# One 112-partition load of wq, and a result finished on 128 partitions with the gate applied last

## The chip, the cores and the metric

The kernel runs on one core of a Trainium2 chip. Five engines work side by side there: TensorE (PE in the profile; PEld is its weight load), VectorE (DVE), ScalarE (ACT), GpSimd (POOL) and SyncE (SP), which here only issues DMAs. The metric is the device time of one execution in microseconds; the time quoted for a kernel is the median of several runs.

## The reference

One token is decoded. An attention block over a long key and value cache and a small MLP mixer both read the same row `x` of 448 numbers, and a scalar gate mixes them:

```python
# x (1,1,448)   k_cache, v_cache (1,8,65536,256)   wq (448,4096)   wo (4096,448)   all bf16
q = (x @ wq).reshape(B, Sq, 16, 256).transpose(0, 2, 1, 3)
k, v = each of the 8 cached heads, used by 2 query heads
p = softmax(einsum("bhqd,bhkd->bhqk", q, k) * 256 ** -0.5)
a = einsum("bhqk,bhkd->bhqd", p, v).transpose(0, 2, 1, 3).reshape(B, Sq, 4096) @ wo
h = layernorm(x);  u = gelu(h (448) x w1 (1792) + b1);  b = u^T @ w2 + b2       # (1,1,448)
g = sigmoid((x * gate_w).sum(-1))
return g * a + (1 - g) * b
```

The caches are 2 x 268 MB, wq and wo 3.67 MB each. The caches are nearly all of the bytes.

## The kernel before

**Tiling.** The 8 heads of 65,536 keys are cut into 32 stages (`NP`) of 16,384 keys, four stages a head. A stage is one K load and one V load of 8.4 MB each, laid out as 128 partitions of 64 KB. K goes into a ring of one and a half stages (`kring`), V into one buffer (`vbuf`). The last K load and the first are cut in two halves, the last V load in four pieces.

**The engines in a stage.** A stage is eight chunks (`BODY`) of 2,048 keys. For each, PE transposes the keys into PSUM (L298), DVE and ACT copy them to SBUF (L569, L669), PE multiplies them with the two query columns (L318), ACT takes the exponential (L658). At the end of the stage PE sums the weights (L347) and multiplies them with V (L358). DVE and ACT also carry one step of the mixer in each of the first 14 stages. At the end of a head DVE takes the sums (`take`, L573 to L583), PE selects and projects with that head's rows of wo (L405) into `prj`, four column groups of 112 on the PSUM partitions 0, 32, 64, 96.

**The order of the DMAs.** SP issues all large loads on one queue, in program order: wq in two parts (L226, L228), K of stage 0 (L231, two halves), then, once q (`s_q`) and the broadcast layer norm (`s_hb`) are ready, V of stage 0 and the first rows of wo (L260). After that each K load waits until the first half of the stage before has been transposed (L237), and each V load until the stage before has finished with the buffer (L250). The last rows of wo go out after the last V pieces (L265). The small inputs come on ACT's queue (L638 to L643).

**wq before.** 448 rows don't divide by 128 partitions. `wq_a` takes the first 384 rows, three whole rows of 8 KB to a partition (24 KB); `wq_b` takes the last 64 rows, each cut in two halves, one half to a partition (4 KB). To match, PE turns `x` into columns `xcol`: three for the whole rows (L427) and two for the half rows, from a zero-padded copy `xrem` that DVE makes (L483, L490, L491, waited for by `s_xrem`). Then 32 column groups of q are each the sum of four matmuls, three of `wq_a` (L441) and one of `wq_b` (L443). wq lies in the V buffer, so V of stage 0 waits for q.

**Gate and mixer before.** `bcast` holds g, 1 - g and b2 on every partition. `take` multiplies the reciprocal of the softmax sum by g (L582), so what is projected is gated already. The mixer's sum gathers in the other half of the `prj` bank; once it is complete, after the seventh head, DVE copies it, adds b2 (L622 to L625), and signals `s_mix`. In the last stage PE waits for that and adds (1 - g) * b into `prj` with four one-row matmuls (L342), ahead of eight matmuls that only keep PE running (`spin`, L334).

**The end before.** After the last projection DVE and ACT copy two of the four column groups each to `out_row` on partition 0 (L634, L678), each copy adding 1 to `s_fin`; SP waits for 4 and writes one row of 896 bytes (L267).

```python
            eng.wait_ge(s_proj, H - 1)
            for h in range(REP):
                w = A_wo[(HQ - REP + h) * DH:(HQ - REP + h + 1) * DH, :]
                eng.dma_start(wo_sb[:, h, :], w.rearrange("(p j) n -> p (j n)", j=2)).then_inc(sem_wl[h], 16)
            eng.wait_ge(s_fin, NCG)
            eng.dma_start(out_ap, out_row[:, :]).then_inc(sem_out, 16)
```

Of the kernel before, what the change touches and what calls it, by code (L numbers as in the profile page):

```python
# [12 lines left out]
def bass_gated_mix__gqa_block_cached__mixer_token_mlp__decode_kernel(  # L13
# [40 lines left out]
    KTB = 2  # L54
    assert T % (CH * BODY) == 0 and PPH >= 2

    WF = 3
    REM = DM - WF * P
    assert 0 < REM and 2 * REM == P
    HALF = NQ // 2  # L60

# [28 lines left out]
    with ctx:  # L92
# [6 lines left out]
        def new_sem(name):  # L99
            return ctx.enter_context(nc.semaphore(name))  # L100
# [19 lines left out]

        early = vbuf[:, :, :].rearrange("p n d -> p (n d)")
        early_f = vbuf_f[:, :, :].rearrange("p n d -> p (n d)")
        wq_a = early[:, 0:WF * NQ].rearrange("p (j n) -> p j n", j=WF)
        wq_b = early[:, WF * NQ:WF * NQ + HALF]
        used = [WF * NQ + HALF]

        def scratch(rows, n, dt=bf16):
            o = used[0]
# [3 lines left out]

        wrows_b = scratch(3 * FT, P)
        identb = scratch(3 * FT, 3 * FT)
        xrem = scratch(1, 2 * P).rearrange("p (a n) -> p a n", a=2)
        xrow_b = scratch(1, DM)
        grow_b = scratch(1, DM)
        xcb_row = scratch(1, DM)
# [4 lines left out]
        scr_row = scratch(1, DM, f32)  # L143
        gu = sb([P, DM], bf16, "gu")
        w2cur = sb([P, 1], bf16, "w2cur")
        xcol = sb([P, WF + 2], bf16, "xcol")
        oTn = sb([P, 2 * REP], bf16, "oTn")
        accs = sb([P, SELC], f32, "accs")
        sel = sb([P, REP], f32, "sel")
# [10 lines left out]
        u_b = sb([P, DM], bf16, "u_b")  # L160
        z_b = sb([P, DM], bf16, "z_b")
        wtmp = sb([P, DM], bf16, "wtmp")
        out_row = sb([1, DM], bf16, "out_row")
        rest = sb([P, 1], bf16, "rest")
        bcast = sb([P, 3], f32, "bcast")
        brow1 = u_b[:, 0:WG]
        brow = z_b[:, 0:WG]
# [29 lines left out]
        s_d2a = new_sem("s_d2a")  # L197
        s_a2d = new_sem("s_a2d")
        s_col = new_sem("s_col")
        s_xrem = new_sem("s_xrem")  # L200
        s_xcol = new_sem("s_xcol")
        s_hrow = new_sem("s_hrow")
        s_h = new_sem("s_h")
# [3 lines left out]
        s_pb = new_sem("s_pb")  # L207
        s_oTn = new_sem("s_oTn")
        s_proj = new_sem("s_proj")
        s_mix = new_sem("s_mix")  # L210
        s_fin = new_sem("s_fin")
        sem_out = new_sem("sem_out")

        block = ctx.enter_context(nc.Block())

        x_row_ap = A_x.rearrange("a b c -> (a b) c")
        out_ap = out.rearrange("a b n -> (a b) n")

        def src(cache, j, n0=0, n1=NV):
            g, m = divmod(j, PPH)  # L220
# [3 lines left out]
        @block.sync  # L224
        def _(eng):
            eng.dma_start(wq_a.rearrange("p j n -> p (j n)"),  # L226
                          A_wq[0:WF * P, :].rearrange("(p j) n -> p (j n)", p=P)).then_inc(sem_wq, 16)
            eng.dma_start(wq_b, A_wq[WF * P:DM, :].rearrange("r (a n) -> (r a) n", a=2)  # L228
                          ).then_inc(sem_wq, 16)
            def load(dst, cache, j, n0, n1, at, sem):  # L230
                eng.dma_start(dst[:, at + n0:at + n1, :].rearrange("p n d -> p (n d)"), src(cache, j, n0, n1)  # L231
                              ).then_inc(sem, 16)

            for j in range(NP):
                last = j == NP - 1
                if j >= 1:
                    eng.wait_ge(sem_tr[NB - 1], BODY * (j - 1) + DC)  # L237
                if j == 0:
                    load(kring, A_k_cache, j, HV, NV, 0, sem_k)
                    load(kring, A_k_cache, j, 0, HV, 0, sem_kb)  # L240
                elif last:
                    load(kring, A_k_cache, j, 0, HV, HV, sem_k)
                    load(kring, A_k_cache, j, HV, NV, HV, sem_kb)
                else:
                    load(kring, A_k_cache, j, 0, NV, HV * (j % 2), sem_k)
                if j == 0:
                    eng.wait_ge(s_q, 1)
                    eng.wait_ge(s_hb, 1)
                else:
                    eng.wait_ge(sem_pv, j)  # L250
                load(vbuf, A_v_cache, j, 0, NFIRST if last else NV, 0, sem_v)
                if last:
                    for (n0, n1), sem in zip(pieces, sem_vp):
                        load(vbuf, A_v_cache, j, n0, n1, 0, sem)
                g, m = divmod(j, PPH)
                if m == 0 and g < H - 1:
                    if g >= 1:
                        eng.wait_ge(s_proj, g)
                    w = A_wo[g * REP * DH:(g + 1) * REP * DH, :]
                    eng.dma_start(wo_rows, w.rearrange("(p i) n -> p (i n)", i=2 * REP)).then_inc(sem_wo, 16)  # L260

            eng.wait_ge(s_proj, H - 1)
            for h in range(REP):
                w = A_wo[(HQ - REP + h) * DH:(HQ - REP + h + 1) * DH, :]
                eng.dma_start(wo_sb[:, h, :], w.rearrange("(p j) n -> p (j n)", j=2)).then_inc(sem_wl[h], 16)  # L265
            eng.wait_ge(s_fin, NCG)
            eng.dma_start(out_ap, out_row[:, :]).then_inc(sem_out, 16)  # L267
            eng.wait_ge(sem_out, 16)

        @block.gpsimd  # L270
# [11 lines left out]
        def _(pe):  # L282
# [53 lines left out]

            def values(j, c0, u16):
                with pe.If(j == NP - 1):
                    pe.wait_ge(s_mix, 1)
                    for q in range(NCG):  # L340
                        r = slice(32 * q, 32 * q + 1)
                        pe.matmul(prj[r, 0:WG], rest[r, :], brow[r, :], start=False, stop=True,  # L342
                                  skip_group_check=True)
                    spin(8)
                pe.wait_ge(sem_exp, c0 + (BODY + 2))
                for r in range(BODY):
# [76 lines left out]
            pe.wait_ge(sem_ident, 1)  # L423
            pe.wait_ge(sem_x, 16)
            for j in range(WF):
                pe.matmul(acc[:, j:j + 1], xrow_b[0:1, j:WF * P:WF], one, start=True, stop=True)
            pe.wait_ge(s_xrem, 2)  # L427
            for a in range(2):
                pe.matmul(acc[:, WF + a:WF + a + 1], xrem[0:1, a, :], one, start=True, stop=True)
            pe.wait_ge(sem_misc, 16 * 5)  # L430
            pe.matmul(acc[:, WF + 2:WF + 2 + 3 * FT], wrows_b, identb, start=True, stop=True).then_inc(s_col, 1)  # L431

            pe.wait_ge(s_xcol, 1)
            pe.wait_ge(sem_wq, 32)
            for dj in range(2):
                for h in range(HQ):
                    j = dj * HQ + h
                    col = h * DH
                    a, cb = divmod(col, HALF)
                    for kt in range(WF):  # L440
                        pe.matmul(sps[:, 1, j:j + 1], wq_a[:, kt, col + dj:col + DH:2],  # L441
                                  xcol[:, kt:kt + 1], start=(kt == 0), stop=False)
                    ins = pe.matmul(sps[:, 1, j:j + 1], wq_b[:, cb + dj:cb + DH:2],  # L443
                                    xcol[:, WF + a:WF + a + 1], start=False, stop=True)
            ins.then_inc(s_q, 1)
            pe.wait_ge(s_hrow, 1)
            pe.matmul(prj[:, 0:DM], ones_sq[0:1, :], h_row, start=True, stop=True)
# [32 lines left out]
        def _(vec):  # L480
            for b in range(0, NB, 2):
                vec.sem_inc(sem_ev[b], 1)
            vec.memset(xrem, 0.0)  # L483
            vec.memset(zrow[:, :], 0.0)
            vec.wait_ge(sem_ident, 1)
            vec.tensor_copy(identb, ident[0:3 * FT, 0:3 * FT]).then_inc(s_xrem, 1)
            vec.reduce_sum(sel[:, :], ident[:, :].rearrange("p (j n) -> p n j", j=4)[:, 0:REP, :], axis=AX.X)
            vec.wait_ge(sem_x, 16)
            vec.drain()
            vec.tensor_copy(xrem[0:1, 0, 0:P:2], xrow_b[0:1, WF * P:DM])  # L490
            vec.tensor_copy(xrem[0:1, 1, 1:P:2], xrow_b[0:1, WF * P:DM]).then_inc(s_xrem, 1)  # L491
            vec.tensor_copy(xrow, xrow_b)
            vec.drain()
            vec.reduce_sum(stat[:, 0:1], xrow, axis=AX.X)
# [19 lines left out]
            vec.drain()  # L514
            vec.tensor_copy(statb[:, 4:5], stat[:, 3:4]).then_inc(s_d2a, 1)
            vec.wait_ge(s_col, 1)
            vec.tensor_copy(xcol[:, :], acc[:, 0:WF + 2]).then_inc(s_xcol, 1)
            vec.tensor_copy(params[:, :], acc[:, WF + 2:WF + 2 + 3 * FT]).then_inc(s_par, 1)
            vec.drain()
            vec.tensor_copy(w2p_b[:, :], params[:, 2 * FT:3 * FT])  # L520
            vec.wait_ge(s_a2d, 1)
# [47 lines left out]
                    vec.tensor_copy(ktT[:, k % KTB, b, :], kst_b[:, b, :]).then_inc(sem_ev[b], 1)  # L569

            def take(n, sem=sem_pv):  # L573
                vec.wait_ge(sem, n)
                vec.tensor_copy(accs[:, :], acc[:, 0:SELC]).then_inc(s_cp, 1)  # L575
                vec.drain()
                vec.reduce_sum(densum[:, :], accs[:, DENC:SELC].rearrange("p (nn hh) -> p hh nn", hh=REP),
                               axis=AX.X)
                vec.drain()
                vec.reciprocal(rden[:, :], densum[:, :])  # L580
                vec.drain()
                vec.tensor_scalar(rden[:, :], rden[:, :], bcast[:, 0:1], None, op0=ALU.mult)  # L582
                vec.drain()  # L583

            def by_head(src):
# [35 lines left out]
            vec.wait_ge(s_proj, H - 1)  # L621
            vec.tensor_copy(brow1, prj[:, WG:2 * WG])  # L622
            vec.drain()
            vec.tensor_copy(rest[:, :], bcast[:, 1:2])
            vec.tensor_scalar(brow, brow1, bcast[:, 2:3], None, op0=ALU.add).then_inc(s_mix, 1)  # L625
            with nc.Fori(NC - NCPH, NC, BODY, engines=on) as c0:
                for k in range(BODY):
                    evacuate(k, c0 + k)
# [1 line left out]
            vec.wait_ge(s_late, 1)  # L630
            by_head(sps[:, 0, 0:2 * REP])
            vec.wait_ge(s_proj, H)
            for q in range(0, NCG, 2):
                vec.tensor_copy(out_row[:, q * WG:(q + 1) * WG], prj[32 * q:32 * q + 1, 0:WG]).then_inc(s_fin, 1)  # L634

        @block.scalar
        def _(act):
# [25 lines left out]
            with nc.Fori(0, NP, 1, engines=OrderedEngineSet([act.engine])) as j:  # L663
# [9 lines left out]
                with act.If(j < FT):  # L673
                    act.wait_ge(s_u, j + 1)
                    act.activation(z_b[:, :], z_b[:, :], AF.Tanh).then_inc(s_tanh, 1)  # L675
            act.wait_ge(s_proj, H)
            for q in range(1, NCG, 2):
                act.activation(out_row[:, q * WG:(q + 1) * WG], prj[32 * q:32 * q + 1, 0:WG], AF.Copy  # L678
                               ).then_inc(s_fin, 1)


# [26 lines left out]
```

## Time and profile before

| what | value |
|---|---|
| median of 3 runs | 1266.1 us (1265.93 to 1266.6) |
| the profiled execution: its own time | 1266.1 us |
| its span, first to last instruction | 1264.0 us |
| bytes read from HBM | 544.22 MB, 431 GB/s over the span |
| busy: PE, PEld, ACT, DVE | 73%, 69%, 43%, 33% |
| second wq load: issued, last data packet ended | 1.20 us, 11.63 us after the span's start |
| first transpose of keys on PE | 27.4 us |
| last rows of wo landed, result's DMA issued | 1261.44 us, 1262.49 us |

A time after the span's start is counted from the first instruction. The profile says for each engine how long it was busy, for each group of instructions what ended the idle time before it, and for the whole span one chain: from the last instruction back to what released it, and so on. DMA packets are recorded one by one, with queue, start, duration and size. A load of 128 partitions shows 128 data packets and 16 packets of 4 bytes, one for each of the 16 DMA engines, that raise the semaphore.

### The profile page before, as it was taken

To read this page: it belongs to the slowest core of one execution; us is meant where nothing else is said; L and a number is where in the kernel's file an instruction comes from. 1 tells how busy PE (TensorE), PEld (TensorE's weight loads), DVE (VectorE), ACT (ScalarE), POOL (GpSimd) and SP (SyncE) were. 2 spreads that over 40 slices of the span, in tenths; PEclk is the share of its full clock that TensorE was granted. 3 is DMA by queue.
4 is the path that set the end of the run, shared out by engine and by line. 5 is a ranking of instruction groups with operands and counts; after the bars stand their busy time and mean duration, and the time that the engine had idled before them with its cause. 6 is when DMAs were issued, how large, how long until landed. Compare 5 with 4: busy or idle time off the path is not lost.

```text
span 1264.0 us, 38850 instructions
## 1 busy us (share of the span) xinstructions
PE 917.0 (73%) x17114; PEld 868.4 (69%) x17114; DVE 422.5 (33%) x764; ACT 538.2 (43%) x788; POOL 0.9 (0%) x7
## 2 busy tenths in 40 slices
PE   3876678766778667786676876758767688676688
PEld 2766668766677666786666876658766578666687
DVE  2433344333444333443222332323322233332233
ACT  1443345533355433454333553335533355433455
POOL 0000000000000000000000000000000000000000
PEclk9887788787898887987888987889887888877999
DMA  9999999999999999999999999999999999999998
GB/s 411 428 434 436 433 431 431 431 438 431 433 433 433 433 431 438 425 433 440 431 436 429 431 431 433 440 433 433 431 431 431 438 436 433 431 433 431 431 427 367
DMA packets 11623, 544.39 MB, mean 431 GB/s; under 512 B 1369, under 2 KB 1628, under 8 KB 2908
## 3 DMA queue, kind: packets, MB, share of 16 engines
q1 hardware_dynamic: 11522, 544.22, 99.7%
q8 instruction: 8, 0.13, 0.0%
q10 hardware_dynamic: 90, 0.01, 0.0%
q14 instruction: 3, 0.02, 0.0%
HBM read 544.22 MB, written 0.00 MB: 431 GB/s over the span
## 4 chain that ended last, share of the span: by engine, by line
DMA 70%; PE 29%; issue 1%; SPq 0%; DVEq 0%; DVE 0%; ACT 0%; ACTq 0%
DMA kring<-in_A_k_cache_dram 68%; PE kst L298 24%; PE sps L318 4%; DMA wo_sb<-in_A_wo_dram 2%; PE acc L358 0%; SPq L231 0%; SPq L265 0%; SPq L228 0%; SPq L226 0%; PE prj L405 0%; PE acc L347 0%; DVEq L92 0%; DVE out_row L634 0%; ACT pT L658 0%; ACTq L658 0%
## 5 line engine op out<-in xcount | busy, mean ns | idle before, releaser
L298 PE MATMUL kst<-ident,kring 128*128 128x128 f32 x4096 | 563.7, 299 | 304.9 <-DMA kring<-in_A_k_cache_dram 294.1
L669 ACT ACTIVATE ktT<-kst 128x1024 bf16<-128x1024 bf16 x512 | 500.0, 1021 | 667.3 <-PE kst L298 666.5
L298 PEld LDWEIGHTS kst<-ident,kring 128*128 128x128 f32 x4096 | 514.0, 156 | 314.8 <-issue 312.2
L569 DVE COPY ktT<-kst 128x1024 bf16<-128x1024 bf16 x512 | 354.2, 692 | 765.0 <-PE kst L298 742.0
L318 PEld LDWEIGHTS sps<-qcur,ktT 128*128 128x128 bf16 x8192 | 237.8, 96 | 4.1 <-issue 1.6
L318 PE MATMUL sps<-qcur,ktT 128*128 128x2 bf16 x8192 | 236.6, 163 | 1.3 <-issue 1.3
L358 PE MATMUL acc<-vbuf,pT 128*2 128x256 bf16 x4080 | 140.4, 305 | 3.8 <-issue 3.3
L358 PEld LDWEIGHTS acc<-vbuf,pT 128*2 128x2 bf16 x4080 | 105.2, 93 | 30.6 <-issue 3.8
L658 ACT ACTIVATE pT<-sps 128x32 f32 x256 | 51.8, 202 | 16.4 <-PE sps L318 16.4
L347 PE MATMUL acc<-pT,ones_sq 128*128 128x32 bf16 x256 | 11.7, 178 | 12.3 <-ACT pT L658 12.3
L347 PEld LDWEIGHTS acc<-pT,ones_sq 128*128 128x128 bf16 x256 | 8.6, 96 | 15.2 <-ACT pT L658 14.9
L675 ACT ACTIVATE z_b<-z_b 128x448 bf16<-128x448 bf16 x14 | 8.1, 577 | 20.5 <-DVE z_b L556 20.4
L575 DVE COPY accs<-acc 128x288 f32<-128x288 f32 x8 | 3.7, 458 | 38.5 <-PE acc L358 38.5
L394 PEld LDWEIGHTS acc<-sel,accs 128*64 128x64 f32 x112 | 10.8, 214 | 0.9
L394 PE MATMUL acc<-sel,accs 128*64 128x1 f32 x112 | 11.4, 260 | 0.0
L431 PE MATMUL acc<-vbuf 42*128 42x42 bf16 x1 | 0.2, 214 | 8.3 <-DMA b_b<-in_B_b_dram 8.3
L405 PE MATMUL prj<-wo_sb,oTn 128*1 128x112 bf16 x128 | 3.7, 244 | 3.1 <-DVE oTn L600 2.9
L431 PEld LDWEIGHTS acc<-vbuf 42*128 42x128 bf16 x1 | 0.1, 102 | 8.4 <-DMA b_b<-in_B_b_dram 8.4
L562 DVE TENSOR_TENSOR gu<-wtmp,z_b 128x448 bf16<-128x448 bf16 x14 | 5.5, 393 | 1.0
L554 DVE TENSOR_TENSOR z_b<-u_b,wtmp 128x448 bf16<-128x448 bf16 x14 | 5.5, 393 | 1.0
L550 DVE TENSOR_TENSOR z_b<-wtmp,u_b 128x448 bf16<-128x448 bf16 x14 | 5.5, 393 | 1.0
L548 DVE TENSOR_TENSOR wtmp<-u_b 128x448 bf16<-128x448 bf16 x14 | 5.5, 392 | 1.1
(89 smaller groups left out, 82.5 us busy)
## 6 DMA issues: line engine op xcount, KB each, us to landing
kring<-in_A_k_cache_dram SPq DMA_DIRECT2D x4, 4096.0 KB, 24.3
vbuf<-in_A_v_cache_dram SPq DMA_DIRECT2D x1, 6144.0 KB, 25.7
wo_sb<-in_A_wo_dram SPq DMA_DIRECT2D x7, 448.0 KB, 27.6
vbuf<-in_A_wq_dram SPq DMA_DIRECT2D x1, 3072.0 KB, 10.2
vbuf<-in_A_v_cache_dram SPq DMA_DIRECT2D x1, 1024.0 KB, 27.8
vbuf<-in_A_v_cache_dram SPq DMA_DIRECT2D x1, 768.0 KB, 28.9
vbuf<-in_A_wq_dram SPq DMA_DIRECT2D x1, 512.0 KB, 10.9
vbuf<-in_A_v_cache_dram SPq DMA_DIRECT2D x31, 29.7
```

The costliest lines, as they stand in the source:

```text
L298: ins = pe.transpose(kst[:, b, i * P:(i + 1) * P], kring_f[:, at + NT * (k % DC) + 4 * b + i, :], ident[:, :])
L318: ins = pe.matmul(sps[:, par, 2 * nt:2 * nt + 2], ktT[:, par, b, ntl * DH + dj:(ntl + 1) * DH:2], qcur[:, dj, :], start=(dj == 0), stop=(d ...
L347: pe.matmul(acc[:, DENC:SELC], ones_sq[:, :], pT[:, r, :], start=False, stop=(r == BODY - 1), skip_group_check=True)
L358: ins = pe.matmul(acc[o:o + REP, 0:DH], pT[:, r, 2 * nt:2 * nt + 2], vbuf[:, n, :], start=False, stop=False, skip_group_check=True)
L394: ins = pe.matmul(dst[hh * HP:(hh + 1) * HP, i:i + 1], accs[:, i:DH:2 * REP], sel[:, hh:hh + 1], start=False, stop=True, skip_group_check= ...
L548: vec.tensor_tensor(W, U, U, op=ALU.mult)
L550: vec.tensor_tensor(Z, W, U, op=ALU.mult)
L554: vec.tensor_tensor(Z, U, W, op=ALU.add)
L569: vec.tensor_copy(ktT[:, k % KTB, b, :], kst_b[:, b, :]).then_inc(sem_ev[b], 1)
L658: act.activation(pT[:, bass.ds(p0 + k % DC, 1), :].rearrange("p o n -> p (o n)"), sps[:, k % 2, 0:2 * NT], AF.Exp, scale=scale).then_inc(s ...
L669: act.activation(ktT[:, k % KTB, b, :], kst_b[:, b, :], AF.Copy).then_inc(sem_ev[b], 1)
L675: act.activation(z_b[:, :], z_b[:, :], AF.Tanh).then_inc(s_tanh, 1)
```

## The change

wq is loaded by one DMA: four whole rows of 8 KB to each of 112 partitions. `xcol` becomes 112 x 4, `xrem` and its two matmuls, its memset and its two copies go, and each q column group is four matmuls over 112 rows. The gate leaves `take`. (1 - g) * b + (1 - g) * b2 is kept on DVE as a float32 tile `run_g` on all 128 partitions, and PE's four one-row matmuls and `s_mix` go. At the end one DVE instruction computes prj * g + run_g for all partitions into `out_g`; ACT does nothing there; SP waits for one signal and writes four rows of 224 bytes from the partitions 0, 32, 64, 96.

```diff
-    WF = 3
-    REM = DM - WF * P
-    HALF = NQ // 2
+    WF = 4
+    PQ = DM // WF
...
             eng.dma_start(wq_a.rearrange("p j n -> p (j n)"),
-                          A_wq[0:WF * P, :].rearrange("(p j) n -> p (j n)", p=P)).then_inc(sem_wq, 16)
-            eng.dma_start(wq_b, A_wq[WF * P:DM, :].rearrange("r (a n) -> (r a) n", a=2)
-                          ).then_inc(sem_wq, 16)
+                          A_wq.rearrange("(p j) n -> p (j n)", j=WF)).then_inc(sem_wq, 16)
...
-            eng.wait_ge(s_fin, NCG)
-            eng.dma_start(out_ap, out_row[:, :]).then_inc(sem_out, 16)
+            eng.wait_ge(s_fin, 1)
+            eng.dma_start(out_ap, out_g[0:P:P // NCG, :]).then_inc(sem_out, 16)
...
                 with pe.If(j == NP - 1):
-                    pe.wait_ge(s_mix, 1)
-                    for q in range(NCG):
-                        r = slice(32 * q, 32 * q + 1)
-                        pe.matmul(prj[r, 0:WG], rest[r, :], brow[r, :], start=False, stop=True,
-                                  skip_group_check=True)
                     spin(8)
...
-                pe.matmul(acc[:, j:j + 1], xrow_b[0:1, j:WF * P:WF], one, start=True, stop=True)
-            pe.wait_ge(s_xrem, 2)
-            for a in range(2):
-                pe.matmul(acc[:, WF + a:WF + a + 1], xrem[0:1, a, :], one, start=True, stop=True)
+                pe.matmul(acc[0:PQ, j:j + 1], xrow_b[0:1, j:DM:WF], one, start=True, stop=True)
+            pe.wait_ge(s_identb, 1)
...
                     for kt in range(WF):
-                        pe.matmul(sps[:, 1, j:j + 1], wq_a[:, kt, col + dj:col + DH:2],
-                                  xcol[:, kt:kt + 1], start=(kt == 0), stop=False)
-                    ins = pe.matmul(sps[:, 1, j:j + 1], wq_b[:, cb + dj:cb + DH:2],
-                                    xcol[:, WF + a:WF + a + 1], start=False, stop=True)
+                        ins = pe.matmul(sps[:, 1, j:j + 1], wq_a[:, kt, col + dj:col + DH:2],
+                                        xcol[:, kt:kt + 1], start=(kt == 0), stop=(kt == WF - 1))
...
                 vec.reciprocal(rden[:, :], densum[:, :])
-                vec.drain()
-                vec.tensor_scalar(rden[:, :], rden[:, :], bcast[:, 0:1], None, op0=ALU.mult)
                 vec.drain()
...
-            vec.tensor_copy(rest[:, :], bcast[:, 1:2])
-            vec.tensor_scalar(brow, brow1, bcast[:, 2:3], None, op0=ALU.add).then_inc(s_mix, 1)
+            vec.tensor_scalar(brow, brow1, bcast[:, 2:3], None, op0=ALU.add)
+            vec.drain()
+            vec.tensor_scalar(run_g[:, :], brow, bcast[:, 1:2], None, op0=ALU.mult)
...
             vec.wait_ge(s_proj, H)
-            for q in range(0, NCG, 2):
-                vec.tensor_copy(out_row[:, q * WG:(q + 1) * WG], prj[32 * q:32 * q + 1, 0:WG]).then_inc(s_fin, 1)
+            vec.scalar_tensor_tensor(out_g[:, :], prj[:, 0:WG], bcast[:, 0:1], run_g[:, :],
+                                     op0=ALU.mult, op1=ALU.add).then_inc(s_fin, 1)
...
-            act.wait_ge(s_proj, H)
-            for q in range(1, NCG, 2):
-                act.activation(out_row[:, q * WG:(q + 1) * WG], prj[32 * q:32 * q + 1, 0:WG], AF.Copy
-                               ).then_inc(s_fin, 1)
```

More of the change, by code (lines that the diff above doesn't have):

```diff
@@ L55, in bass_gated_mix__gqa_block_cached__mixer_token_mlp__decode_kernel @@
     assert T % (CH * BODY) == 0 and PPH >= 2
-    WF = 3
-    REM = DM - WF * P
-    assert 0 < REM and 2 * REM == P
-    HALF = NQ // 2
+    WF = 4
+    PQ = DM // WF
+    assert PQ * WF == DM and PQ <= P and PQ % 16 == 0
     NFIRST = 96
@@ L122, in bass_gated_mix__gqa_block_cached__mixer_token_mlp__decode_kernel @@
         early_f = vbuf_f[:, :, :].rearrange("p n d -> p (n d)")
-        wq_a = early[:, 0:WF * NQ].rearrange("p (j n) -> p j n", j=WF)
-        wq_b = early[:, WF * NQ:WF * NQ + HALF]
-        used = [WF * NQ + HALF]
+        wq_a = early[0:PQ, 0:WF * NQ].rearrange("p (j n) -> p j n", j=WF)
+        used = [WF * NQ]
         def scratch(rows, n, dt=bf16):
@@ L134, in bass_gated_mix__gqa_block_cached__mixer_token_mlp__decode_kernel @@
         identb = scratch(3 * FT, 3 * FT)
-        xrem = scratch(1, 2 * P).rearrange("p (a n) -> p a n", a=2)
         xrow_b = scratch(1, DM)
@@ L145, in bass_gated_mix__gqa_block_cached__mixer_token_mlp__decode_kernel @@
         w2cur = sb([P, 1], bf16, "w2cur")
-        xcol = sb([P, WF + 2], bf16, "xcol")
+        xcol = sb([PQ, WF], bf16, "xcol")
         oTn = sb([P, 2 * REP], bf16, "oTn")
@@ L162, in bass_gated_mix__gqa_block_cached__mixer_token_mlp__decode_kernel @@
         wtmp = sb([P, DM], bf16, "wtmp")
-        out_row = sb([1, DM], bf16, "out_row")
-        rest = sb([P, 1], bf16, "rest")
+        run_g = sb([P, WG], f32, "run_g")
+        out_g = sb([P, WG], bf16, "out_g")
         bcast = sb([P, 3], f32, "bcast")
@@ L199, in bass_gated_mix__gqa_block_cached__mixer_token_mlp__decode_kernel @@
         s_col = new_sem("s_col")
-        s_xrem = new_sem("s_xrem")
+        s_identb = new_sem("s_identb")
         s_xcol = new_sem("s_xcol")
@@ L209, in bass_gated_mix__gqa_block_cached__mixer_token_mlp__decode_kernel @@
         s_proj = new_sem("s_proj")
-        s_mix = new_sem("s_mix")
         s_fin = new_sem("s_fin")
@@ L216, in bass_gated_mix__gqa_block_cached__mixer_token_mlp__decode_kernel @@
         x_row_ap = A_x.rearrange("a b c -> (a b) c")
-        out_ap = out.rearrange("a b n -> (a b) n")
+        out_ap = out.rearrange("a b (q n) -> (a b q) n", q=NCG)
         def src(cache, j, n0=0, n1=NV):
@@ L425, in _ @@
             for j in range(WF):
-                pe.matmul(acc[:, j:j + 1], xrow_b[0:1, j:WF * P:WF], one, start=True, stop=True)
-            pe.wait_ge(s_xrem, 2)
-            for a in range(2):
-                pe.matmul(acc[:, WF + a:WF + a + 1], xrem[0:1, a, :], one, start=True, stop=True)
+                pe.matmul(acc[0:PQ, j:j + 1], xrow_b[0:1, j:DM:WF], one, start=True, stop=True)
+            pe.wait_ge(s_identb, 1)
             pe.wait_ge(sem_misc, 16 * 5)
-            pe.matmul(acc[:, WF + 2:WF + 2 + 3 * FT], wrows_b, identb, start=True, stop=True).then_inc(s_col, 1)
+            pe.matmul(acc[:, WF:WF + 3 * FT], wrows_b, identb, start=True, stop=True).then_inc(s_col, 1)
             pe.wait_ge(s_xcol, 1)
-            pe.wait_ge(sem_wq, 32)
+            pe.wait_ge(sem_wq, 16)
             for dj in range(2):
@@ L438, in _ @@
                     col = h * DH
-                    a, cb = divmod(col, HALF)
                     for kt in range(WF):
-                        pe.matmul(sps[:, 1, j:j + 1], wq_a[:, kt, col + dj:col + DH:2],
-                                  xcol[:, kt:kt + 1], start=(kt == 0), stop=False)
-                    ins = pe.matmul(sps[:, 1, j:j + 1], wq_b[:, cb + dj:cb + DH:2],
-                                    xcol[:, WF + a:WF + a + 1], start=False, stop=True)
+                        ins = pe.matmul(sps[:, 1, j:j + 1], wq_a[:, kt, col + dj:col + DH:2],
+                                        xcol[:, kt:kt + 1], start=(kt == 0), stop=(kt == WF - 1))
             ins.then_inc(s_q, 1)
@@ L482, in _ @@
                 vec.sem_inc(sem_ev[b], 1)
-            vec.memset(xrem, 0.0)
             vec.memset(zrow[:, :], 0.0)
             vec.wait_ge(sem_ident, 1)
-            vec.tensor_copy(identb, ident[0:3 * FT, 0:3 * FT]).then_inc(s_xrem, 1)
+            vec.tensor_copy(identb, ident[0:3 * FT, 0:3 * FT]).then_inc(s_identb, 1)
             vec.reduce_sum(sel[:, :], ident[:, :].rearrange("p (j n) -> p n j", j=4)[:, 0:REP, :], axis=AX.X)
@@ L489, in _ @@
             vec.drain()
-            vec.tensor_copy(xrem[0:1, 0, 0:P:2], xrow_b[0:1, WF * P:DM])
-            vec.tensor_copy(xrem[0:1, 1, 1:P:2], xrow_b[0:1, WF * P:DM]).then_inc(s_xrem, 1)
             vec.tensor_copy(xrow, xrow_b)
@@ L516, in _ @@
             vec.wait_ge(s_col, 1)
-            vec.tensor_copy(xcol[:, :], acc[:, 0:WF + 2]).then_inc(s_xcol, 1)
-            vec.tensor_copy(params[:, :], acc[:, WF + 2:WF + 2 + 3 * FT]).then_inc(s_par, 1)
+            vec.tensor_copy(xcol[:, :], acc[0:PQ, 0:WF]).then_inc(s_xcol, 1)
+            vec.tensor_copy(params[:, :], acc[:, WF:WF + 3 * FT]).then_inc(s_par, 1)
             vec.drain()
```

## The prediction

> **What bounds the kernel now.** First the page: the DMA row of the 40 slices, the queue that moved the bytes, and the chain that ended last.
>
> ```profile
> DMA  9999999999999999999999999999999999999998
> q1 hardware_dynamic: 11522, 544.22, 99.7%
> ## 4 chain that ended last, share of the span: by engine, by line
> DMA 70%; PE 29%; issue 1%; SPq 0%; DVEq 0%; DVE 0%; ACT 0%; ACTq 0%
> ```
>
> The DMA engines are busy from the first slice to the last, with one queue's packets. The windows say whether "busy" means full:
>
> ```profile
> 0.00:12.00 12.00, 0.64 (x6) 0.39 (x6) 4.63 (x18) 1.28 (x1) 0.91 (x7) 1.00 0.89 351
> 12.00:24.00 12.00, 4.69 (x132) 3.87 (x132) 2.65 (x15) 1.69 (x3) 0.00 (x0) 1.00 1.01 436
> 48.00:1250.00 1202.00, 880.63 (x16411) 835.77 (x16410) 402.51 (x710) 518.28 (x758) 0.00 (x0) 0.84 1.00 433
> ```
>
> The last columns are DMA share and GB/s. In the packet records a 64 KB packet takes 2.420 us in the median, which is 27.08 GB/s; sixteen such engines (I call them lanes) make 433.3 GB/s, and the long window shows 433. So no lane idles from 48 to 1250 us: the time is the bytes of the slowest lane plus a head and a tail. Anything that costs the lanes time, wherever it sits, arrives at the end one for one; anything on another engine costs nothing until it starves them. That shows where to look: at the start, where wq is loaded, at SP's issues, and at the tail. The timeline of the start:
>
> ```profile
> 0.74 0.41 SPq L226 DMA_DIRECT2D vbuf<-in_A_wq_dram  x1
> 1.20 0.41 SPq L228 DMA_DIRECT2D vbuf<-in_A_wq_dram  x1
> 11.08 0.21 PE L431 MATMUL acc<-vbuf 42*128 42x42 bf16 x1 [8.33 <-DMA b_b<-in_B_b_dram]
> 12.37 0.17 DVE L517 CAST xcol<-acc 128x5 bf16<-128x5 f32 x1
> 15.99 0.17 PE L443 MATMUL sps<-xcol,vbuf 128*128 128x1 bf16 x1
> 17.54 0.33 SPq L231 DMA_DIRECT2D vbuf<-in_A_v_cache_dram  x1
> 38.79 0.33 SPq L231 DMA_DIRECT2D kring<-in_A_k_cache_dram  x1
> ```
>
> Data starts to move at 1.76 us, q is done at about 16.2, V of stage 0 goes out at 17.54 and the second K load at 38.79. And the tail, from the chain and the timeline:
>
> ```profile
> 1232.11 29.33 DMA wo_sb<-in_A_wo_dram
> 1261.49 0.39 PE prj L405 x6
> 1261.90 0.26 DVE out_row L634
> ```
> ```profile
> 1252.58 0.21 PE L342 MATMUL prj<-z_b,rest 1*1 1x112 bf16 x4
> 1255.34 3.23 PE L358 MATMUL acc<-vbuf,pT 128*2 128x256 bf16 x112 [0.51 <-DMA vbuf<-in_A_v_cache_dram]
> 1260.74 0.16 DVE L588 TENSOR_TENSOR oTn<-sps,rden 128x4 bf16<-128x4 f32 x1 [0.84 <-PE sps L379]
> 1261.90 0.54 ACT L678 ACTIVATE out_row<-prj 1x112 bf16<-1x112 f32 x2 [8.90 <-PE prj L405]
> 1261.90 0.56 DVE L634 CAST out_row<-prj 1x112 bf16<-1x112 f32 x2 [1.00 <-PE prj L405]
> 1262.49 0.32 SPq L267 DMA_DIRECT2D out_dram<-out_row  x1
> ```
>
> The last rows of wo land at 1261.44, one projection follows, the copies, the result's DMA, and the span ends at 1264.0. The profiled execution took 1266.1 us, so 2.1 lie outside its span; it equals the median, so the sum starts at 1266.1.
>
> **The tail, part by part.** The two copies on each of two engines lie on the path: 0.56 us. One instruction over 128 x 112 takes their place. The nearest rows: L622, 128 x 112 out of PSUM, 0.27 us; L625, the same shape by a per-partition scalar, 0.24; L548, two tensors of 128 x 448, 0.39. I take 0.30, between 0.24 and 0.39: a gain of 0.26 (0.17 to 0.32). The result goes out in four rows of 224 bytes; the 896-byte packet took 40 ns, ACT's 256-byte ones 18 each, and SP's issues cost 0.32 to 0.44, so between 0 and 4 x 18 - 40 ns + 0.12 = 0.15 is added. I take 0, as four rows can go to four lanes at once. The four matmuls L342 (0.21 us) go, but PE then waits longer for the last V load (0.51 us at L358 becomes 0.7): nothing. The g product L582 (0.23 us, 8 times) goes. In the tail DVE waits 0.84 us for PE at L588 anyway; at the seven other head ends it stands ahead of the wo load that SP issues, with 8 us and more of packets queued before the lanes would notice. The new run_g product (a row like L625, 0.24, less 0.16 for the copy L624) runs at 1119, and DVE's next copy waits for K that lands at 1124.7: 5 us of cover; without it, 0.1.
>
> **The start on the compute engines.** Gone: a memset (0.17) and two copies (0.20, 0.19) on DVE, two tiny matmuls on PE. Both then waited for the small inputs until 11.05 us, so nothing is gained. q stays at 32 x 4 matmuls. Cover for a late q: at 17.54 the lanes hold wq and K of stage 0, 12.06 MB, until 1.76 + 12.06 / 0.4333 = 29.6 us, so 12 us. The second K load at 38.79 has all of wq, K, V and wo rows before it, 20.9 MB, until 50.0: 11 us of cover. A start that is up to 10 us later on PE costs nothing; if that cover were gone, every us late would cost one. One issue less on SP lets K go out 0.46 us earlier into lanes that are full until 11.6 anyway: nothing. No wait is added on any queue; those for s_mix, s_xrem and ACT's for the projection vanish.
>
> **The wq load on the lanes.** This is the only term that can move the time by more than a few tenths. Before, each lane had eight packets of 24 KB (0.912 us each) and eight of 4 KB (0.159): 8.57 us. After, if 112 rows are dealt evenly, each lane has seven packets of 32 KB; the halves of the first and last K loads have packets of that size, 1.213 us: 8.49 us. That is the lower end, -0.08 us. It assumes that a packet runs at full speed wherever its rows lie. The trace of before can't show that: in all its large loads the lanes share 128 partitions eight each, and all of them run at full speed. If it is the partitions that are tied to lanes, eight each, 112 of them keep only fourteen busy, with 8 x 1.213 = 9.70 us: +1.1. If rows are dealt in sevens to lanes and each group of eight partitions takes bytes no faster than one lane's rate, the runs of seven don't match the groups of eight, lanes meet at a group and share its rate, and it is more. The farthest row for lanes in each other's way are the first sixteen packets of wq: 1.07 to 2.17 us, median 1.635, in place of 0.912, a factor 1.79 (part of it the start of the stream). Seven packets at 1.79 x 1.213 make 15.2 us: +6.7, the upper end. Between -0.08 and +6.7 neither row is nearer; I take the middle, +3.3, since a run of seven lies partly in a group it shares and partly in one that it has for itself.
>
> [...]
>
> The sum: 1266.1 + 3.3 - 0.26 = 1269.1 us.
>
> **The rivals.** Differences of up to 0.2% (2.5 us) I call the same, about what a measurement of this kernel can tell from no change.
>
> *The lanes don't care about partitions.* Then 1266.1 - 0.08 - 0.26 = 1265.8. For it: every packet of one size takes the same time to 1% in the whole trace; against: all those are 128-partition loads. It decides from packets of 1.21 us each throughout the wq load. This is the case on the other side, not slower.
>
> *Fourteen of sixteen groups, perfectly kept busy*: 1266.1 + 1.1 - 0.26 = 1266.9, also the same. For it: it needs only that eight partitions belong to a lane. Against: 112 divides by 16, so the even deal is the plain one.
>
> *Worse than a factor 1.79.* If neighbouring rows go to neighbouring lanes, four at a time in one group, packets run at a quarter: 8.49 x 3 = +25 us, 1291. Likewise if the load runs on fewer lanes: seven with sixteen rows each would take 19.4 us, +10.8 on them, 1276.7. Against both: nothing in the before trace runs that slowly.
>
> *Faster by over 2.5 us* has no mechanism: even the whole lane time of the 4 KB packets (8 x 0.159 = 1.27) and all of the tail copies (0.56) make only 1.8.
>
> **How the numbers follow.** Forecast 0.50; no effect of partitions 0.22; fourteen groups 0.13; far worse 0.12; faster 0.03. The forecast's own range is 1267.6 to 1272.5 (1266.1 + 6.7 - 0.26), and most of it lies beyond 1268.6. The range that should hold the time 8 times in 10 reaches down to the no-effect case with the tail's best gain, 1265.6, and up to 1272.6; it leaves out the far-worse case and the faster one, 0.15. Slower by over 0.2%: nearly all of the forecast and the far-worse case, 0.60; the same 0.37; faster 0.03.
>
> **What would show it.** In the changed kernel's trace: the 32 KB packets of wq longer than the 1.21 us of K's halves, by about 1.4 times in the mean; lanes ending the wq load several us apart; under 400 GB/s from 12 to 24 us or less than 351 in the first 12; then 433 again, and the last wo rows landing about 3 us later than 1261.44. The tail shows one DVE instruction of about 0.3 us between the last projection and SP's issue. Wrong would be: packets at 1.21 us and a landing at 1261.4 (no effect), or a rate below 433 after 48 us (something I don't see).

## The result and the profile after

1271.7 us (median of 6 runs, 1271.47 to 1271.93) against 1266.14 before (6 runs): a ratio of 1.0044, 95% interval 1.0031 to 1.0057. The kernel became 5.6 us slower. The profiled execution took 1271.93 us with a span of 1270.1.

The windows of the changed kernel, with the columns as before (at the end of each line granted clock, DMA share, GB/s):

```profile
0.00:12.00 12.00, 0.55 (x4) 0.49 (x4) 3.42 (x13) 1.28 (x1) 0.91 (x7) 1.00 0.93 246
12.00:24.00 12.00, 0.27 (x4) 0.19 (x5) 1.31 (x5) 0.17 (x1) 0.00 (x0) 1.00 0.97 342
48.00:1250.00 1202.00, 890.99 (x16519) 841.49 (x16517) 403.60 (x707) 521.90 (x765) 0.00 (x0) 0.84 1.00 433
```

The lanes are as "busy" as before, at 0.93 and 0.97, but move 246 and 342 GB/s where the kernel before moved 351 and 436. From 48 us on the rate is 433 in both. So a share of 0.93 or 0.97 said here that packets were open, not that they moved at full speed.

How much was lost, and when, can be worked out from the packet records: take the bytes that the large-load queue has moved by a time t, divide by 433.3 GB/s, and subtract from t. I call it the lag; it is a mean over the sixteen lanes.

| lag in us at | 6 | 12 | 20 | 48 | 72 | 84 | 1250 |
|---|---|---|---|---|---|---|---|
| before | 2.8 | 2.9 | 2.9 | 3.3 | 3.7 | 3.7 | 3.8 |
| after | 3.5 | 5.8 | 8.4 | 8.8 | 9.2 | 9.4 | 9.4 |

At 20 us the changed kernel is 5.5 us behind, at the end 5.6. All but 0.1 us of it is lost while wq is loaded. The first 112 packets of 32 KB took 2.11 us in the median, where those of the same size in K's halves before took 1.213. No lane was spared: the sixteen 4-byte packets that close the load, one on each lane, started between 15.33 and 17.19 us; those of the second wq load before, between 11.07 and 11.62. The page's list of DMA issues gives that load's time to landing (the last number), 17.5 us, where the second of the two loads before landed 10.9 us after its issue:

```profile
vbuf<-in_A_wq_dram SPq DMA_DIRECT2D x1, 3584.0 KB, 17.5
```

The timeline shows what else became late:

```profile
22.52 0.38 DVE L493 TENSOR_TENSOR vbuf<-vbuf 1x448 bf16<-1x448 bf16 x1 [16.78 <-DMA b_b<-in_B_b_dram]
28.87 0.33 SPq L226 DMA_DIRECT2D vbuf<-in_A_v_cache_dram  x1
50.21 0.33 SPq L226 DMA_DIRECT2D kring<-in_A_k_cache_dram  x1
73.85 0.33 SPq L226 DMA_DIRECT2D vbuf<-in_A_v_cache_dram  x1
```

The small inputs on ACT's queue seem to wait behind the packets of the large loads: the last four packets there started 1.22 to 1.24 us apart, about the time of one 32 KB packet (1.21 us); that is read from the times, not tested. The work that waits for the last of them starts at 22.52 in place of 11.05 us; q, V of stage 0, the second K and the second V load follow 10 to 11.5 us late (the loads were issued at 17.54, 38.79 and 63.58 before). Here that cost next to nothing, as the lag shows (from 20 to 84 us it rises by 1.0 us, by 0.8 before), but it was close. Last the tail:

```profile
1267.40 0.27 PE L395 MATMUL prj<-wo_sb,oTn 128*1 128x112 bf16 x8 [0.22 <-DMA wo_sb<-in_A_wo_dram]
1267.72 0.33 DVE L613 SCALAR_TENSOR_TENSOR out_g<-prj,bcast,run_g 128x112 bf16<-128x112 f32 x1 [0.93 <-PE prj L395]
1268.09 0.65 SPq L262 DMA_DIRECT2D out_dram<-out_g  x1
```

The one DVE instruction takes 0.33 us in place of 0.56, but SP needs 0.65 us to issue the four-row DMA in place of 0.32, and its first packet starts 1.24 us after the issue began, in place of 0.75. The four packets took 14 ns each and started within 0.06 us.

### The profile page after: what moved, and what is told of

It reads as the page before. It is cut to its first block, busy times and chain, and to the rows that moved or that the text cites. A ratio compares the mean times of both kernels' runs of the same rounds, so it can differ in the third digit from the quotient of the medians.

```text
span 1270.1 us, 38819 instructions
## 1 busy us (share of the span) xinstructions
PE 921.5 (73%) x17109; PEld 868.6 (68%) x17109; DVE 419.9 (33%) x752; ACT 536.9 (42%) x786; POOL 0.9 (0%) x7
## 4 chain that ended last, share of the span: by engine, by line
DMA 69%; PE 29%; issue 1%; DVE 0%; ACTq 0%; SPq 0%; ACT 0%; DVEq 0%
DMA kring<-in_A_k_cache_dram 66%; PE kst L293 24%; PE sps L313 4%; DMA wo_sb<-in_A_wo_dram 2%; DMA b_b<-in_B_b_dram 2%; PE acc L348 0%; PE sps L428 0%; SPq L226 0%; ACTq L621 0%; DVE hbT L588 0%; DVE stat L495 0%; ACTq L618 0%; PE prj L432 0%; SPq L260 0%; DVE vbuf L493 0%
## 5 line engine op out<-in xcount | busy, mean ns | idle before, releaser
L348 PE MATMUL acc<-vbuf,pT 128*2 128x256 bf16 x4080 | 148.9, 316 | 2.3 <-issue 1.5
L348 PEld LDWEIGHTS acc<-vbuf,pT 128*2 128x2 bf16 x4080 | 109.6, 96 | 33.0 <-issue 2.0
## 6 DMA issues: line engine op xcount, KB each, us to landing
vbuf<-in_A_wq_dram SPq DMA_DIRECT2D x1, 3584.0 KB, 17.5
```

The lines of the kernel that those rows point to most:

```text
L348: ins = pe.matmul(acc[o:o + REP, 0:DH], pT[:, r, 2 * nt:2 * nt + 2], vbuf[:, n, :], start=False, stop=False, skip_group_check=True)
```

## The experiments

**Which half of the change.** The kernel before with the load alone, and with the gate and result alone; the edits in outline:

```diff
-  wq_a: A_wq[0:384] to 128 x 3 rows;  wq_b: A_wq[384:448] to 128 half rows
+  wq_a: A_wq to 112 x 4 rows, xcol 112 x 4                        # e1_load_only
-  copies to out_row, g in take, (1 - g) * b by PE
+  scalar_tensor_tensor(out_g, prj, g, run_g), 4-row result DMA    # e2_tail_only
```

> The kernel before with only the 112-partition load of wq (its xcol and matmuls to match); gate, mixer and result as before. If the load is the whole loss: about 1266.1 + 5.9 (the lag of the last wo landing, 1267.36 against 1261.44) = 1272.0, or 1271.4 to 1272.2. If half or more of the loss came from the new gate and result: below 1269.

> The kernel before with only the gate, mixer and result of the change; wq in two loads to 128 partitions. By the prediction's term (copies 0.56 us against one instruction of 0.30): 1265.8. Rival, read from the changed kernel's trace: SP's issue takes 0.65 in place of 0.32 us and the first packet of the result starts 1.24 in place of 0.75 us after it, which eats the gain: 1266.1 to 1266.4.

The load alone: 1271.6 us (1271.14 to 1273.82), ratio 1.0047 [1.0033, 1.0061]: the whole loss. Its lag is 7.7 at 20 us (4.8 more than before) and rises by 1.4 between 72 and 84 us, where the second V load, issued at 74.67, finds the lanes just run dry (367 GB/s from 72 to 84 us, 421 before). The tail alone: 1266.47 us, ratio 1.0004 [0.9995, 1.0013]. The interval holds 1, though all 11 runs (from 1266.4) lie above all 15 of the kernel before (up to 1266.25). There is no gain; if anything it costs 0.4 us, about what the rival said (0 to 0.3).

**One DMA, but 128 partitions.** In outline:

```diff
-  A_wq[0:384] -> 128 x (3 rows);  A_wq[384:448] -> 128 x (half a row)
+  A_wq flat -> 128 x (7 half rows);  x zero-padded for both halves, 14 columns, 7 matmuls a group
```

> The kernel before, but wq comes in one DMA to all 128 partitions, seven half rows (28 KB) each, with a zero-padded x for both halves (14 columns) and 7 matmuls in place of 4 per column group; gate and result as before. If the 112 partitions are the cause (lanes meet on groups of partitions): every packet at 28,672 / 27.0 = 1.06 us, eight to a lane, wq done by 11.6 us, 1266.1. If it is the one large load of wq at the start of the stream, its bytes a lane or where it reads in memory: packets well over 1.3 us and 1270 or more.

1272.35 us (1270.15 to 1272.92), ratio 1.0044 [1.0031, 1.0058]. The load was as expected, the time was not. The windows:

```profile
0.00:12.00 12.00, 0.88 (x14) 0.82 (x14) 4.66 (x16) 1.28 (x1) 0.90 (x7) 1.00 0.87 351
12.00:24.00 12.00, 5.89 (x208) 5.70 (x208) 2.48 (x12) 1.69 (x3) 0.00 (x0) 1.00 1.01 433
48.00:54.00 6.00, 6.00 (x105) 5.90 (x104) 2.96 (x5) 4.31 (x8) 0.00 (x0) 1.00 0.85 310
72.00:78.00 6.00, 5.36 (x96) 3.40 (x89) 0.00 (x0) 0.00 (x0) 0.00 (x0) 0.59 0.43 147
```

Packets of 1.062 us, wq done at 11.92, 351 GB/s as before, a lag of 2.7 at 20 us: here one large load was no slower than two. But from 72 to 78 us the lanes moved 147 GB/s, at a DMA share of 0.43: here they really were empty. The chain of waits tells why:

```profile
24.88 0.48 PE prj L440
...
26.59 14.12 issue
40.71 6.39 PE kst L294 x32
```

q was later (the work that waits for the small inputs started at 15.3 us in place of 11.05, and there are 224 matmuls in place of 128), and PE then stood for 14 us ahead of its first transpose with nothing in the profile to wait for (4.3 us in the kernel before, 9.8 in the changed one). Around that time the records show single 16 KB packets on the instruction queue, 6 to 9 us apart (at 21.9, 30.5 and 37.9 us; at 18.7, 24.6 and 30.6 before). The first transpose started 2.8 us after one of them started in all three kernels (40.71 after 37.9 here, 27.41 after 24.58 before, 39.03 after 36.21 in the changed one). PE seems to have waited for its program; that is read from the times, not tested. So this run shows two costs apart: none for the load, 7 us of lag for a late start.

**A late start alone.**

```diff
             pe.wait_ge(s_xcol, 1)
+            for _ in range(48): pe.matmul(kst[:, NB - 1, :], ones_sq, hot, ...)
```

> The kernel before with 48 idle matmuls of 512 columns on PE between xcol and q (some 11 us), so that V of stage 0 and the second K load are issued about 11 us late, as in the changed kernel (28.87 and 50.21 us); it computes the same. If a late start is covered by what the lanes have queued: 1266.1, up to 1266.6. If the late start on PE is what costs: 1270 and more, with a gap in the DMA rate between 24 and 60 us.

1271.35 us (1268.75 to 1272.33), ratio 1.004 [1.0025, 1.0055]. A start as late as that of the changed kernel cost 2.7 to 6.3 us here, on its own and unsteadily. SP's issues:

```profile
29.73 0.33 SPq L232 DMA_DIRECT2D vbuf<-in_A_v_cache_dram  x1
50.33 0.33 SPq L232 DMA_DIRECT2D kring<-in_A_k_cache_dram  x1
72.02 0.33 SPq L232 DMA_DIRECT2D vbuf<-in_A_v_cache_dram  x1
```

The lag rises by 1.0 at 30 us, 1.2 at 54 and 1.1 between 72 and 80: each of the three loads came as the lanes ran out. In the profiled execution (1270.46 us) that mean over the lanes ends 3.1 us above the kernel before, but the last packet of data comes 4.3 us later: the lanes had also fallen out of step. PE's granted clock was lower there too (0.72 from 24 to 48 us, 1.00 before), which may have made some of the lateness of these issues; that was not tested. In the changed kernel the same issues were about as late, but the slow wq load had put off by 5.5 us the time at which the lanes would run out. The loss there hid the second loss.

**The load by itself, away from the start.** An extra load that nobody reads, from wq into the free end of the K ring, is queued behind K of stage 0; the second K load, which overwrites that place, waits for it. All else is as before.

```diff
+  more = kring[0:128, NV:NV + HV, :]   # then 0:112, 0:64, 32:96, 0:96, 16:128; 28 KB a partition for 128, else 32 KB
+  eng.dma_start(more, wq...).then_inc(sem_more, 16)
+  if j == 1: eng.wait_ge(sem_more, 16)      # ahead of the second K load
```

> The kernel before with one more load behind K of stage 0, which nobody reads: all of wq again, 128 partitions of 28 KB, into the free end of the K ring. Its start is as before, and the lanes have 8.5 us more to do. Every theory: packets of 1.06 us, 1266.1 + 8.5 = 1274.6, less what gaps it fills (1274 to 1275).

> The same extra load to 112 partitions of 32 KB: the changed load by itself, in the middle of the stream, with no engine waiting for it. If 112 partitions are slow for the lanes wherever the load stands: packets of 1.8 to 2.2 us, 5.5 us more than with 128 partitions, 1279.5 to 1281. If it was the start of the stream, or the small loads and the late start of PE beside it: packets of 1.21 us and 1274.6.

> The same place, 64 partitions of 32 KB (2.1 MB, four packets a lane). If only the lanes count: 4 x 1.213 = 4.9 us, 1271. If groups of partitions are shared and 64 partitions give half of them: packets of 2.4 us, 9.7 us, 1275.8. If what matters is that lanes don't get eight partitions, and not which: a factor of 1.7 as with 112, 8.3 us, 1274.4.

> The extra load of 64 partitions again, now the partitions 32 to 95 in place of 0 to 63: the same bytes, rows, packets and lanes. [...] If it is which partitions the lanes meet on: packets of 1.21 us, 1266.1 + 4.85 = 1271.0. If it is how many partitions, or that a lane gets fewer than eight: packets of 2.56 us as with 0 to 63, 1278.8.

> The extra load with 96 partitions (0 to 95) of 32 KB, six packets a lane, 7.3 us at full speed, so 1273.4 if it cost nothing more. If lanes meet on groups of partitions, in runs of six: a mean packet near 1.6 to 2.0 us and some lanes 7 us late, 1278 to 1281. If 112 is slow because a run of seven is odd, and even runs are not: 1273.4.

> The extra load of 112 partitions, 16 to 127 in place of 0 to 111. Runs of seven cross the groups in the same way: 1280 to 1284 beside 1282.3 for 0 to 111. If the price hangs on a few unlucky partitions at the low end: below 1279.

| extra load | full speed | measured over before | not explained by full speed | median packet, against full |
|---|---|---|---|---|
| 128 partitions | 8.5 | 8.45 | 0 | 1.06 / 1.06 |
| 112 (0 to 111) | 8.5 | 16.2 | 7.7 | 2.04 / 1.21 |
| 112 (16 to 127) | 8.5 | 16.95 | 8.5 | 2.2 / 1.21 |
| 96 (0 to 95) | 7.3 | 15.5 | 8.2 | 2.3 / 1.21 |
| 64 (0 to 63) | 4.85 | 12.7 | 7.85 | 2.56 / 1.21 |
| 64 (32 to 95) | 4.85 | 4.75 | 0 | 1.21 / 1.21 |

(us; times over 1266.1 for the first, second and fifth row, 1266.16 for the others. The packets are those of the extra load, taken by size and time; a few of K's halves are among them.) Three times came out above what was expected: 112 partitions from 0 at 1282.3 against at most 1281, 96 at 1281.7 against at most 1281, 64 from 0 at 1278.8 against 1275.8 for half speed. The windows, first of 0 to 111, then of 0 to 63, then of 32 to 95:

```profile
30.00:36.00 6.00, 6.00 (x103) 5.94 (x102) 3.46 (x5) 4.92 (x7) 0.00 (x0) 1.00 1.08 259
36.00:42.00 6.00, 6.00 (x107) 5.92 (x105) 2.77 (x4) 4.62 (x8) 0.00 (x0) 1.00 1.01 264
```
```profile
30.00:36.00 6.00, 6.00 (x68) 5.99 (x67) 2.88 (x5) 3.98 (x6) 0.00 (x0) 1.00 1.16 249
```
```profile
30.00:36.00 6.00, 6.00 (x68) 5.99 (x67) 2.78 (x5) 4.07 (x5) 0.00 (x0) 1.00 1.16 494
```

The last two lines are the same load, the same 64 rows of 32 KB, to other partitions: 249 against 494 GB/s (a rate is booked when its packets start, so short windows overshoot). Between these two it is not how many partitions, not the size of packets and not the source, but which partitions the bytes go to. Packets of 2.56 us are a little slower than half speed (2 x 1.213 = 2.43). That 32 to 95 would run at full speed no run had shown before this one. The ranges 0 to 95 and 0 to 111 contain 32 to 95, yet they cost about as much as 0 to 63 (8.2 and 7.7 us against 7.85; 209 GB/s for 0 to 95 from 36 to 42 us, 264 for 0 to 111). What sets 32 to 95 apart from the slow ranges no trace shows. The lanes that were already on V of stage 0 suffered too: in the run with the 0 to 63 load, 22 of the 64 KB packets took over 2.5 us, against 8 in the kernel before; sixteen of them lie between 40.0 and 44.1 us, up to 4.9 us long. That makes 1.8 of the 7.3 us that the lag grew, and fits a place that lanes share better than slow lanes; where that would be no trace shows.

**The four-row result alone.**

```diff
-  DVE and ACT copy two column groups each to out_row; 1 row of 896 bytes
+  vec.tensor_copy(out_g, prj[:, 0:WG]);                4 rows of 224 bytes
```

> The kernel before with gate and mixer as they were, but the result copied by one DVE instruction over 128 partitions and written from four partitions, 224 bytes each. If the four-row DMA is what costs in the tail: SP's issue at 0.65 us, the first packet 1.2 us after it, 1266.3 to 1266.5 although the copies are 0.3 us shorter. If it is the gate's instruction (0.33 us) or the mixer's: 1265.8.

1266.14 us against 1266.1, ratio 1.0001 [0.9992, 1.001]. The issue took 0.65 us and the first packet started 1.25 us after it began, as expected, the copy took 0.27; cost and gain cancel, and the expectation of 1266.3 to 1266.5 missed. What sets the further 0.3 us of the tail alone apart from this run isn't settled: the spans of the two profiled executions differ by only 0.1 (1264.3 and 1264.2), and it is at the edge of what these runs can tell.

No version here beats the kernel before.

## Why the prediction came out as it did

The time lay within the stated range, 2.6 us above the sum: 1271.7 against 1269.1.

**What bounds the kernel** held: lanes full, and the time lost on them arrived one for one: lag 5.6, time 5.6.

**The wq term** had the right direction and cause (the partitions that the rows go to) and the wrong size: +3.3 was the middle of -0.08 and +6.7 (+6.6, if it is counted from the 8.57 us before like the other end), and 5.5 was measured on the lanes. The failed step is "a run of seven lies partly in a group it shares and partly in one that it has for itself". Runs and groups were the author's picture: no record names a packet's lane or a group of partitions. The packets say otherwise: 2.11 us in the median, 1.74 times full speed (1.67 in the mean, never below 1.39 us), against the factor 1.4 that was forecast; and the lanes did not end "several us apart" but within 1.9 us, all of them late. The upper row, the factor 1.79 of the first sixteen packets, was the nearer one, but by luck: those packets went to 128 partitions, and nothing shows that they were slow for the same reason.

How the lanes are dealt the 112 rows no trace shows, and why 112 cost 5.5 us at the start (4.8 with the load alone) but 7.7 in the middle of the stream isn't settled; there the slow packets of V add 0.8.

**The tail term** was wrong: a gain of 0.26 was put down, and none came. The failed step is "I take 0, as four rows can go to four lanes at once": SP's issue itself doubled from 0.32 to 0.65 us, above the 0.44 that bounded it, and the first packet started 1.24 in place of 0.75 us after the issue began. The instruction was well priced (0.30, measured 0.33).

**The cover** was called 12 and 11 us, and "a start that is up to 10 us later on PE costs nothing" was too sure. It left out the second V load. In the kernel before, SP issues it at 63.58 us (second line, from the timeline), and the K load ahead of it lands at 38.79 + 34.06 = 72.9 (first line, from the chain):

```profile
38.79 34.06 DMA kring<-in_A_k_cache_dram
63.58 0.33 SPq L231 DMA_DIRECT2D vbuf<-in_A_v_cache_dram  x1
```

That is 9.3 us at most, and 5.8 by the sum that gave 12 and 11 (29.3 MB from 1.76 us on): the smallest of the three. The prediction left out too that the small inputs could come late beside a slow load: the last of them took 19.71 us from its issue, about 8.3 before. The late start of 10 to 11.5 us was not forecast at all: the work behind the small inputs was taken to start at 11.05 as before, and started at 22.52. In the changed kernel it stayed just covered; alone it did not.

**The rivals.** Lanes that don't care about partitions (1265.8) are ruled out by 249 against 494 GB/s. Fourteen groups kept perfectly busy (1266.9) would have shown packets of 1.21 us on fourteen lanes; there were none before 17.6 us. What spoke for the first rival, "every packet of one size takes the same time to 1%", was read too strictly: 8 of the 7,808 packets of 64 KB in the trace before took 2.8 to 3.06 us in place of 2.42, and the first of wq were slow as the prediction itself says. The far-worse cases did not come. The other steps at nothing (PE's four matmuls, g in `take`, `run_g`) can hide no more than the 0.3 us of the tail alone that isn't settled; one SP issue less can't be told apart from the slow load.

## What to carry to other kernels

In this kernel, whose DMA queue is always full, the shape of a load counted, though it was 3.7 MB of 544: away from the start, 112 and 96 partitions cost 7.7 to 8.5 us beyond full speed, 128 none. So in a kernel like it try all 128 partitions first, even at the price of a ragged second load, and measure before taking 96 or 112. Slow packets hid here in a busy share of 0.93 and 0.97; look at GB/s and at the time of packets of one size. Cover has to be counted for every later load that depends on the work made late, and the smallest counts (here 12, 11 and 5.8 us).

## What the runs showed that was not expected

The same bytes for 64 partitions ran at full or at half speed by the range alone (0 to 63 against 32 to 95). 112 partitions were nearly as slow as 64: 259 against 249 GB/s in the same window. The last small load on another queue took 19.7 in place of about 8.3 us from its issue while the slow load ran. And the slow load covered a late start: undoing the one without the other (128 partitions in one DMA, with more matmuls behind it) left the time where it was, at 1272.35 against 1271.7 us.
